# Top-32 attention with an ELU feed-forward block: issuing in the written order in place of the scheduler's, with key and query transposes cut into three parts

## The chip, the cores and the metric

The kernel runs on one core of a Trainium2 chip. Five engines work in parallel, each through its own queue, in order: TensorE (PE, matmuls and transposes; PEld is its weight load), VectorE (DVE), ScalarE (ACT), GpSimd (POOL) and SyncE (SP), which here only issues DMAs. An engine waits where the instruction at the head of its queue waits for a semaphore; nothing behind it can pass. The metric is the device time of the core in microseconds, the median of several executions.

## The reference

```python
def _attn_ref(q, k, v):                      # 8 batches, 8 heads, 576 positions, 64 dims
    scores = scale * np.matmul(q, k.transpose(0, 1, 3, 2))
    kth = np.partition(scores, -32, axis=-1)[..., -32:-31]
    scores = np.where(scores >= kth, scores, -1000000000.0)
    scores = scores - np.max(scores, axis=-1, keepdims=True)
    attn = np.exp(scores)
    attn = attn / (np.sum(attn, axis=-1, keepdims=True) + 1e-09)
    return np.matmul(attn, v)

def _moe_ref(x, w_in, w_out):                # x: 4608 x 512; w_in 512 x 2048, w_out 2048 x 512
    h = x @ w_in
    g = np.where(h > 0.0, h, np.exp(np.minimum(h, 0.0)) - 1.0)
    return g @ w_out
```

In every row of 576 scores only the 32 largest go into the softmax. The two weight matrices arrive as 64-bit floats, which the kernel itself turns into 32-bit ones.

## The kernel before, in words

**Steps.** The attention is cut into 144 steps. A step is one tile of 128 query rows and one pair of heads, so two rows of scores per partition, 128 x 576 each (18 steps per batch: eight for each pair of query tiles, two for the 64 rows left over). What a step needs is spread over several turns of the main loop (L569 to L614). In turn n the code writes down: `scores` of step n+2 (PE matmuls L269, ACT evictions L277); `select` of step n, once for each of its two rows (L281); `mask` of step n-1 (L302); `turn` of step n-2, the transposes of its probabilities (L332); and, where a group of two steps is done, `attend` (L354). `normalise` of step n-1 (L319) stands near the end of the turn. Steps 0 to 7 (`tight`) have a loop of their own, in which a step is masked in its own turn.

**Select** is the work of VectorE: for each of the two rows four MAX8 (L287 and L297, the next eight largest) and three MATCH_REPLACE8 (L291, which strike them out), each reading what the one before it wrote. The two rows have a work tile each (`wk`, two buffers).

**Mask and normalise.** GpSimd negates the 32nd largest value (`neg`, L311) and forms `gap`; ScalarE runs Prelu (L314) and Exp with a running sum (L315); GpSimd adds a small number to the sum (`dene`, L324), VectorE takes the reciprocal (`rec`, L326) and GpSimd multiplies both rows by it (L328).

**Feed-forward.** Rows are gathered into 18 blocks of 128, 256 or 384 rows. A block is 16 `hidden` pieces (L414: matmuls, ScalarE Relu and Exp, and later one VectorE operation, the gate L405) and four `project` pieces per 128 rows. `feed` (L530) is called four times in a step and pops pieces by a planner: each has a cost, each block has a due time, and the work is spread evenly over the steps. `feed` first closes the gates of the pieces popped before, so a gate stands a quarter of a step behind its matmuls. The last block can only start when the last step is attended.

**Decoding of the weights.** 32 pieces of 512 KB are loaded through three `raw` buffers. `hook` (L189), called twice in each select, runs one piece: `convert_first` (three ScalarE operations, L165 to L167, and a GpSimd clamp, L168) and `convert_last` of the piece before it (two VectorE operations, L175 and L178, and a GpSimd sum, L182). Blocks other than the first wait for all 32 pieces.

**Order.** What is written down is not the order in which the engines issue. A scheduler, which runs when the program is built, takes the instructions with their dependences and a model of their costs and sets up each engine's queue. So it can pull an instruction ahead of others that were written before it: in the queue of VectorE it runs the two rows of a select side by side, and it lets a `select` begin ahead of the decoding that was written before it.

Keys and queries are loaded per head pair and turned by `transpose_qk` (L234: ten transposes and three ScalarE copies), 5, 3, 1 and -1 steps ahead of a batch's first step.

Of the kernel before, what the change touches and what calls it, by code (L numbers as in the profile page):

```python
# [10 lines left out]
FP32 = mybir.dt.float32  # L11
# [69 lines left out]
def kernel(  # L81
# [10 lines left out]
    P = nc.NUM_PARTITIONS  # L92
# [7 lines left out]
    NC = dm // P  # L100
    NF = dff // P
    NG = NF // 2
    T = 3 * P
# [14 lines left out]
    xtpool = pool("xt", 2)  # L118
# [5 lines left out]
    late = {}  # L124
# [30 lines left out]
    def convert_first(i):  # L155

        lo, hi, e, m = parts(raw[i])
        ef, mf = e.bitcast(FP32), m.bitcast(FP32)
        nc.scalar.activation(ef, hi.bitcast(FP32), AF.Abs, scale=2.0**-48)  # L165
        nc.scalar.activation(mf, lo, AF.Copy, scale=2.0**-29, bias=2.0**23)
        nc.scalar.activation(m.bitcast(I32), mf, AF.Copy, bias=-(2.0**23))  # L167
        nc.gpsimd.tensor_scalar(  # L168
            ef, ef, (2.0 - 2.0**-3 - 2.0**-23) * 2.0**-32, 2.0**-63, ALU.min, ALU.max
        )  # L170
# [18 lines left out]
    def hook():  # L189

        if not decode:
            return
        decode.pop(0)()
        if not decode:
            raws.close()
            late["g"] = ctx.enter_context(tc.tile_pool(name="g", bufs=2))

    def decode_piece(i):
        if i < 2 * NF:
            if i + 2 < 2 * NF:  # L200
                load_weight(i + 2)
            convert_first(i)
        if i > 0:
            convert_last(i - 1)
            decoded[0] = i

    loaded, kqT, vT = {}, {}, {}

    def load_qk(b, hp):
        for name, src in (("k", k), ("q", q)):  # L210
            t = ldpool.tile([P, J + 1, 2, D], FP32, tag=name + "in", name=name + "in")
            for hh in range(2):
                nc.sync.dma_start(
                    t[:, 0:J, hh, :],
                    src[b, 2 * hp + hh, 0:JP, :].rearrange("(p j) d -> p j d", j=J),
                )
            nc.sync.dma_start(
                t[0:R, J, :, :],
                src[b, 2 * hp : 2 * hp + 2, JP:S, :].rearrange("h p d -> p h d"),
            )  # L220
            loaded[b, hp, name] = t
# [10 lines left out]
        vT[b, hp] = t  # L232

    def transpose_qk(b, hp):  # L234
        d = kvpool.tile([P, 2, S], FP32, tag="kqT", name="kqT")
        kqT[b, hp] = d
        srcs = [loaded.pop((b, hp, name)) for name in ("k", "q")]
        for i, src in enumerate(srcs):
            ps = ps_t.tile([P, JP], FP32, tag="t", name="qkps")
            for c in range(J):  # L240
                nc.tensor.transpose(
                    ps[:, c * P : (c + 1) * P],
                    src[:, c, :, :].rearrange("p h d -> p (h d)"),
                    ident[:],
                )
            nc.scalar.copy(d[:, i, 0:JP], ps[:])
        ps = ps_t.tile([P, JP], FP32, tag="t", name="qkps")
        for i, src in enumerate(srcs):
            nc.tensor.transpose(
                ps[:, i * R : (i + 1) * R],  # L250
                src[0:R, J, :, :].rearrange("p h d -> p (h d)"),
                ident[0:R, 0:R],
            )
        nc.scalar.copy(
            d[:, :, JP:S], ps[:, 0 : 2 * R].rearrange("p (a s) -> p a s", a=2)
        )

    def scores(u):
        q0 = u.t.qt * P
# [42 lines left out]
    def mask(u, i):  # L302

        if u.masked:
            return
        if i == 0:
            u.den = small.tile([P, 2], FP32, tag="den", name="den")
        u.masked = i == 1
        sc, low, top = u.sc[:, i, :], u.last[:, i, 7:8], u.first[:, i, 0:1]
        neg = small.tile([P, 1], FP32, tag="neg", name="neg")  # L310
        nc.gpsimd.tensor_scalar_mul(neg[:], low, -1.0)  # L311
        gap = small.tile([P, 1], FP32, tag="gap", name="gap")
        nc.gpsimd.tensor_tensor(gap[:], low, top, ALU.subtract)
        nc.scalar.activation(sc, sc, AF.Prelu, bias=neg[:], alpha=STEEP)  # L314
        nc.scalar.activation(  # L315
            sc, sc, AF.Exp, bias=gap[:], accum_out=u.den[:, i : i + 1]
        )
# [14 lines left out]
    def turn(u, chunks):  # L332

        if u.turned:
            return
        g = u.group
        if g.et is None:
            g.et = etpool.tile([P, 2 * J + 1, len(g.tiles), P], FP32, tag="et", name="et")
        ps = ps_t.tile([P, JP], FP32, tag="t", name="eps")
        sc = u.sc[:, :, :].rearrange("p i s -> p (i s)")  # L340
        n = chunks.stop - chunks.start
        for c in range(n):
            c0 = (chunks.start + c) * P
            nc.tensor.transpose(ps[:, c * P : (c + 1) * P], sc[:, c0 : c0 + P], ident[:])  # L344
        nc.scalar.copy(  # L345
            g.et[:, chunks, u.at, :],
            ps[:, 0 : n * P].rearrange("p (c q) -> p c q", c=n),
        )
        if chunks.stop == 2 * J + 1:
            u.turned = True  # L350
            if u.at == len(g.tiles) - 1:
                closing.append(g)
# [38 lines left out]

    def finish(blk, parts, at, cols, src):
        if blk.xT is None:
            blk.xT = xtpool.tile([P, NC, T], FP32, tag="xT", name="xT")
        nc.scalar.copy(blk.xT[:, at, cols], src)  # L395
        blk.left -= parts
        if blk.left == 0:
            ffn.extend(ffn_pieces(blk))
# [117 lines left out]
    def at(step, fn, *args):  # L516
        todo.setdefault(step, []).append((fn, args))

    for b in range(1, B):
        f = first[b]  # L520
        for hp, (ahead, ready, late_v) in enumerate(
            ((7, 5, 2), (5, 3, -2), (3, 1, -2), (1, -1, -3))
        ):
            at(f - ahead, load_qk, b, hp)
            at(f - ready, transpose_qk, b, hp)
            at(f - late_v, load_v, b, hp)

    fed = {"at": 0.0, "sum": 0.0, "over": 0.0}
# [1 line left out]
    def feed(n, share):  # L530

        close_gates()
        fed["at"] = max(fed["at"], n)
        ahead = [(w - fed["sum"]) / (x - fed["at"]) for x, w in due if x > fed["at"]]
        if ahead:
            fed["over"] += max(0.0, share * min(ahead))
        fed["at"] += share
        while ffn and decoded[0] >= ffn[0][1] and 0.5 * ffn[0][0] <= fed["over"]:
            cost, _, piece = ffn.pop(0)
            fed["over"] -= cost  # L540
            fed["sum"] += cost
            piece()

    load_qk(0, 0)
    for i in range(2):
        load_weight(i)
    load_qk(0, 1)
    load_v(0, 0)
    transpose_qk(0, 0)
    scores(steps[0])  # L550
    load_qk(0, 2)
    transpose_qk(0, 1)
    scores(steps[1])
    load_qk(0, 3)
    for hp in range(1, NHP):
        load_v(0, hp)
    decode += [lambda i=i: decode_piece(i) for i in range(2 * NF + 1)]
    at(0, transpose_qk, 0, 2)
    at(1, transpose_qk, 0, 3)

    def step(n):
        return steps[n] if 0 <= n < NS else None
# [6 lines left out]
    for n in range(NS + 3):  # L569
        for fn, args in todo.pop(n, []):  # L570
            fn(*args)
        ahead, cur, prev, done = step(n + 2), step(n), step(n - 1), step(n - 2)
        if ahead:
            scores(ahead)
        if n < tight:
            for i in range(2):
                passes = choose(n, i)
                next(passes)
                if i == 0:
                    while closing:  # L580
                        attend(closing.pop(0))
                elif prev:
                    normalise(prev)
                    turn(prev, slice(0, J))
                    turn(prev, slice(J, J + 1))
                    turn(prev, slice(J + 1, 2 * J + 1))
                feed(n, 0.25)
                next(passes)
                mask(cur, i)
                feed(n, 0.25)  # L590
            continue
        if prev:
            mask(prev, 0)
        passes = choose(n, 0)
        next(passes)
        feed(n, 0.25)
        while closing:
            attend(closing.pop(0))
        next(passes)
        feed(n, 0.25)  # L600
        if prev:
            mask(prev, 1)
        if done:
            turn(done, slice(0, J))
            turn(done, slice(J, J + 1))
        passes = choose(n, 1)
        next(passes)
        feed(n, 0.25)
        if done:
            turn(done, slice(J + 1, 2 * J + 1))  # L610
        next(passes)
        if prev:
            normalise(prev)
        feed(n, 0.25)  # L614
# [36 lines left out]
```

## Time and profile before

| | |
|---|---|
| device time, median of 3 | 1848.46 us (1846.58 to 1849.24) |
| span of the profiled execution | 1845.9 us, 25773 instructions |
| VectorE | 1580.3 us busy, 3376 instructions |
| ScalarE | 1125.8 us busy, 2473 instructions |
| GpSimd | 416.6 us busy, 1078 instructions |
| DMA | 56.20 MB, a mean of 30 GB/s |
| MAX8, L287 and L297 | 1152, 837.2 us in sum |
| MATCH_REPLACE8, L291 | 864, 639.0 us in sum |
| gates, L405 | 288, 117.6 us in sum |

Sums of busy time overlap: on VectorE one instruction's record runs on by some 0.08 us after the next has started, so time is best read from start to start. The first MAX8 starts at 16.3 us, that of step 8 at 148.6, of step 48 at 570.6, of step 72 at 849.8 and of step 143 at 1715.6; the last select ends at 1727.1. What follows, 119 us, is feed-forward work alone.

### The profile page before, as it was taken

The numbers are of one execution on the slowest core, as the hardware profiler recorded it, in microseconds if no ns is written. First come the engines' busy times: TensorE is split into PE (matmuls) and PEld (weight loads), VectorE is DVE, ScalarE is ACT, GpSimd is POOL, SyncE is SP. The second block draws the span as 40 slices with busy tenths as digits, with TensorE's granted clock in tenths as the row PEclk, the third lists the DMA queues.
The fourth block names the chain that finished last, engine by engine and source line by source line (L and its number), as shares of the span: only waits on it lengthen the run. The fifth ranks groups of instructions, "written<-read, shape, count | busy, mean of one in ns | idle before, by whom it ended". The sixth has DMA issues, their size and how long they took to land.

```text
span 1845.9 us, 25773 instructions
## 1 busy us (share of the span) xinstructions
PE 1698.4 (92%) x8352; PEld 1025.0 (56%) x8352; DVE 1580.3 (86%) x3376; ACT 1125.8 (61%) x2473; POOL 416.6 (23%) x1078
## 2 busy tenths in 40 slices
PE   5478899999999999999989999999999999899999
PEld 3245656474665655555456565645546465555555
DVE  6889999999999989989889798988989888998400
ACT  5786766676766666667556575657656475665421
POOL 2663222222222221212222221221222212121100
PEclk7579999999999999999999999999999999999999
DMA  5530120001000120001100101001100000000000
GB/s 159 167 126 30 26 56 2 12 20 45 26 7 7 32 58 7 7 24 41 26 12 1 38 23 41 1 12 39 33 19 6 19 20 26 6 7 7 1 18 12
DMA packets 101126, 56.20 MB, mean 30 GB/s; under 512 B 84096, under 2 KB 92288, under 8 KB 100992
## 3 DMA queue, kind: packets, MB, share of 16 engines
q1 hardware_dynamic: 100992, 54.55, 10.6%
q8 instruction: 67, 1.10, 0.2%
q14 instruction: 67, 0.55, 0.1%
HBM read 45.09 MB, written 9.44 MB: 30 GB/s over the span
## 4 chain that ended last, share of the span: by engine, by line
DVE 59%; PE 17%; ACT 12%; issue 3%; POOL 2%; DMA 0%; POOLq 0%; ACTq 0%
DVE wk L291 25%; DVE m L297 22%; DVE m L287 8%; PE hps L425 6%; PE ops L443 6%; ACT sc L314 4%; DVE gT L405 3%; ACT sc L315 3%; ACT sc L277 2%; PE scps L269 2%; PE avps L371 2%; PE eps L344 1%; POOL neg L311 1%; ACT n L434 1%; ACT n L433 1%
## 5 line engine op out<-in xcount | busy, mean ns | idle before, releaser
L297 DVE MAX8 m<-wk 128x8 f32<-128x576 f32 x864 | 628.2, 750 | 4.6
L425 PE MATMUL hps<-xT,w_in 128*128 128x256 f32 (+2 forms) x2304 | 573.5, 395 | 27.8 <-DVE gT L405 26.9
L443 PE MATMUL ops<-w_out,gT 128*128 128x512 f32 x1152 | 535.3, 604 | 1.8 <-DVE gT L405 1.8
L425 PEld LDWEIGHTS hps<-xT,w_in 128*128 128x128 f32 x2304 | 405.5, 196 | 142.4 <-DVE gT L405 45.6
L291 DVE MATCH_REPLACE8 wk<-m,wk 128x576 f32<-128x576 f32 x576 | 426.3, 742 | 0.0
L314 ACT ACTIVATE sc<-sc,neg 128x576 f32<-128x576 f32 x288 | 223.3, 775 | 276.8 <-POOL neg L311 275.6
L443 PEld LDWEIGHTS ops<-w_out,gT 128*128 128x128 f32 x1152 | 208.1, 192 | 208.1 <-issue 199.7
L345 ACT COPY et<-eps 128x512 f32<-128x512 f32 (+1 forms) x432 | 193.5, 476 | 153.5 <-PE eps L344 153.3
L269 PE MATMUL scps<-kqT 64*128 64x64 f32 (+3 forms) x1280 | 244.1, 461 | 25.0 <-ACT sc L277 24.3
L344 PE MATMUL eps<-ident,sc 128*128 128x128 f32 x1296 | 208.0, 284 | 49.3 <-ACT xT L395 16.4
L344 PEld LDWEIGHTS eps<-ident,sc 128*128 128x128 f32 x1296 | 159.6, 144 | 162.3 <-issue 55.2
L311 POOL TENSOR_SCALAR neg<-m 128x1 f32<-128x1 f32 x288 | 62.0, 215 | 831.1 <-DVE m L297 830.0
L328 POOL TENSOR_SCALAR sc<-sc,rec 128x576 f32<-128x576 f32 x288 | 215.7, 759 | 138.9 <-DVE rec L326 130.9
L287 DVE MAX8 m<-sc 128x8 f32<-128x576 f32 x288 | 209.0, 748 | 31.6 <-ACT sc L277 29.6
L315 ACT ACTIVATE sc<-sc,gap 128x576 f32<-128x576 f32 x288 | 223.1, 775 | 16.7 <-ACT sc L314 1.1
L291 DVE MATCH_REPLACE8 wk<-m,sc 128x576 f32<-128x576 f32 x288 | 212.7, 742 | 0.0
L371 PE MATMUL avps<-et,vT 128*64 128x256 f32 (+5 forms) x2000 | 205.5, 337 | 7.0 <-ACT et L345 6.6
L405 DVE SCALAR_TENSOR_TENSOR gT<-n,hps 128x256 f32<-128x256 f32 (+2 forms) x288 | 117.6, 409 | 106.0 <-ACT n L434 104.8
L433 ACT ACTIVATE n<-hps 128x256 f32<-128x256 f32 (+2 forms) x288 | 109.4, 380 | 149.2 <-PE hps L425 146.3
L269 PEld LDWEIGHTS scps<-kqT 64*128 64x128 f32 (+1 forms) x1280 | 114.7, 184 | 143.7 <-issue 109.7
L277 ACT ACTIVATE sc<-scps 128x576 f32<-128x576 f32 x288 | 171.3, 640 | 11.1 <-PE scps L269 11.0
L371 PEld LDWEIGHTS avps<-et,vT 128*64 128x64 f32 (+1 forms) x2000 | 114.0, 140 | 97.4 <-issue 42.2
(34 smaller groups left out, 722.4 us busy)
## 6 DMA issues: line engine op xcount, KB each, us to landing
kin<-in_k_dram SPq DMA_DIRECT2D x64, 128.0 KB, 2.8
qin<-in_q_dram SPq DMA_DIRECT2D x64, 128.0 KB, 2.8
raw<-in_moe_w_in_dram SPq DMA_DIRECT2D x16, 512.0 KB, 4.1
vT<-in_v_dram SPq DMA_DIRECT2D x64, 128.0 KB, 2.3
raw<-in_moe_w_out_dram SPq DMA_DIRECT2D x16, 512.0 KB, 3.2
out_dram<-osb SPq DMA_DIRECT2D x32, 256.0 KB, 2.2
kin<-in_k_dram SPq DMA_DIRECT2D x32, 32.0 KB, 2.5
qin<-in_q_dram SPq DMA_DIRECT2D x32, 32.0 KB, 2.5
```

Source lines behind the costliest of these rows:

```text
L269: nc.tensor.matmul(ps[rows, start[i] : start[i] + keys.stop - keys.start], kq[part, 1, q0 : q0 + u.t.ql], kq[part, 0, keys], start=True, s ...
L277: nc.scalar.activation(u.sc[:, i, :], ps[:, first[i] : first[i] + S], AF.Copy, scale=scale)
L287: nc.vector.max(m, sc)
L291: nc.vector.match_replace(wk[:], m, cur, TAKEN)
L297: nc.vector.max(m, cur)
L314: nc.scalar.activation(sc, sc, AF.Prelu, bias=neg[:], alpha=STEEP)
L315: nc.scalar.activation(sc, sc, AF.Exp, bias=gap[:], accum_out=u.den[:, i : i + 1])
L328: nc.gpsimd.tensor_scalar(u.sc[:, i, :], u.sc[:, i, :], rec[:, i : i + 1], 1.0, ALU.mult, ALU.mult)
L344: nc.tensor.transpose(ps[:, c * P : (c + 1) * P], sc[:, c0 : c0 + P], ident[:])
L371: nc.tensor.matmul(ps[i * D : (i + 1) * D, cols], vt[rows, 2 * J if c == J else i * J + c, :], w, start=(c == 0), stop=(c == J),)
L425: nc.tensor.matmul(ps[:, 0:n_tok], w_in[:, i, f * P : (f + 1) * P], blk.xT[:, i, 0:n_tok], start=(i == 0), stop=(i == NC - 1),)
L443: nc.tensor.matmul(blk.o[:], blk.gT[f // NG][:, f % NG, s * P : (s + 1) * P], w_out[:, f, :], start=(f == 0), stop=(f == NF - 1),)
```

## The change

Four engines (PE, ACT, DVE and POOL) are taken out of the scheduler's hands and issue in the order in which the code is written; SP's queue is still scheduled. The rest of the change fits the written order to that. `transpose_qk` becomes a generator in three parts, of which one is written down at each of three places in a step, one step earlier than before, so that the transposes do not stand in one lump in PE's queue. In `decode_piece` the sum of the piece before is written ahead of the clamp of the next. A block of 128 rows takes its `xT` tile from a pool of its own once decoding is over, so that no copy waits for a block that is written later.

```diff
     def decode_piece(i):
         if i < 2 * NF:
             if i + 2 < 2 * NF:
                 load_weight(i + 2)
-            convert_first(i)
         if i > 0:
             convert_last(i - 1)
             decoded[0] = i
+        if i < 2 * NF:
+            convert_first(i)
...
             nc.scalar.copy(d[:, i, 0:JP], ps[:])
+            yield
...
+    def start_qk(b, hp):
+        turning.append(transpose_qk(b, hp))
+
+    def turn_qk(whole=False):
+        while turning:
+            if next(turning[0], turning) is turning:
+                turning.pop(0)
+            elif not whole:
+                return
...
         if blk.xT is None:
-            blk.xT = xtpool.tile([P, NC, T], FP32, tag="xT", name="xT")
+            if blk.slots == 1 and late:
+                blk.xT = late["x"].tile([P, NC, P], FP32, tag="xT", name="xT")
+            else:
+                blk.xT = xtpool.tile([P, NC, T], FP32, tag="xT", name="xT")
...
-            ((7, 5, 2), (5, 3, -2), (3, 1, -2), (1, -1, -3))
+            ((8, 6, 2), (5, 4, -2), (3, 2, -2), (2, 0, -3))
         ):
             at(f - ahead, load_qk, b, hp)
-            at(f - ready, transpose_qk, b, hp)
+            at(f - ready, start_qk, b, hp)
...
+    E = mybir.EngineType
+    ctx.enter_context(
+        tc.manual_schedule(engines={E.PE, E.Activation, E.DVE, E.Pool})
+    )
...
+        if n < tight:
+            turn_qk(True)
         if ahead:
             scores(ahead)
...
         feed(n, 0.25)
+        turn_qk()
         while closing:
             attend(closing.pop(0))
...
             mask(prev, 1)
+        turn_qk()
...
             turn(done, slice(J + 1, 2 * J + 1))
+        turn_qk()
```

More of the change, by code (lines that the diff above doesn't have):

```diff
@@ L196, in hook @@
             late["g"] = ctx.enter_context(tc.tile_pool(name="g", bufs=2))
+            late["x"] = ctx.enter_context(tc.tile_pool(name="x", bufs=1))
     def decode_piece(i):
@@ L256, in transpose_qk @@
         )
+        yield
+    def start_qk(b, hp):
[6 more added lines that the diff above has]
+                return
+    turning = []
     def scores(u):
@@ L548 @@
     load_v(0, 0)
-    transpose_qk(0, 0)
+    start_qk(0, 0)
+    turn_qk(True)
     scores(steps[0])
     load_qk(0, 2)
-    transpose_qk(0, 1)
+    start_qk(0, 1)
+    turn_qk(True)
     scores(steps[1])
@@ L557 @@
     decode += [lambda i=i: decode_piece(i) for i in range(2 * NF + 1)]
-    at(0, transpose_qk, 0, 2)
-    at(1, transpose_qk, 0, 3)
+    at(0, start_qk, 0, 2)
+    at(1, start_qk, 0, 3)
     def step(n):
@@ L572 @@
         ahead, cur, prev, done = step(n + 2), step(n), step(n - 1), step(n - 2)
+        if n < tight:
+            turn_qk(True)
         if ahead:
```

## The prediction

> **What bounds the kernel now.** I began with the page's first two parts: which engine is full, and when.
>
> ```profile
> PE 1698.4 (92%) x8352; PEld 1025.0 (56%) x8352; DVE 1580.3 (86%) x3376; ACT 1125.8 (61%) x2473; POOL 416.6 (23%) x1078
> ...
> PE   5478899999999999999989999999999999899999
> ...
> DVE  6889999999999989989889798988989888998400
> ```
>
> Both look full, and VectorE stops some 120 us before the end. But a matmul's record is longer than its slot: the group of `hps` 128x256 has a mean of 392 ns, and in the trace one starts 216 ns after the other. Counts by start-to-start times make PE's work about 1520 us (hps 499, ops 494, transposes 176, `avps` 184, `scps` 170). PE has room.
>
> Second, the windows (columns: window, length, then PE, PEld, DVE, ACT, POOL busy, clock, DMA):
>
> ```profile
> 400.00:600.00 200.00, 193.48 (x955) 117.63 (x954) 196.65 (x440) 130.68 (x297) 45.97 (x133) 1.00 0.08 21
> ...
> 1200.00:1400.00 200.00, 190.13 (x854) 104.86 (x853) 174.87 (x364) 118.27 (x248) 40.66 (x117) 0.96 0.09 25
> ...
> 1700.00:1800.00 100.00, 99.35 (x384) 56.21 (x383) 29.04 (x61) 35.13 (x77) 6.30 (x16) 1.00 0.03 9
> ```
>
> Up to step 48 VectorE hardly waits; later it idles one eighth of the time; the end is PE alone. In steps (first MAX8 of each): 10.55 us a step from 8 to 48, 11.63 from 48 to 72, 12.19 from 72 to 143.
>
> Third, VectorE's timeline (start, duration, instruction), because the change touches its order:
>
> ```profile
> 903.97 0.74 DVE L291 MATCH_REPLACE8 wk<-m,wk 128x576 f32<-128x576 f32 x1
> 904.63 0.08 DVE L291 MATCH_VALUE_LOAD wk<-m,wk 128x8 f32 x1
> 904.70 0.74 DVE L291 MATCH_REPLACE8 wk<-m,wk 128x576 f32<-128x576 f32 x1
> 905.36 1.41 DVE L297 MAX8 m<-wk 128x8 f32<-128x576 f32 x2
> 906.80 0.09 DVE L291 MATCH_VALUE_LOAD wk<-m,wk 128x8 f32 x1
> 906.88 0.74 DVE L291 MATCH_REPLACE8 wk<-m,wk 128x576 f32<-128x576 f32 x1
> 907.66 0.76 DVE L297 MAX8 m<-wk 128x8 f32<-128x576 f32 x1
> ```
>
> The scheduler pairs the two rows of a select. Where the neighbours are of different rows, replace to MAX8 takes 0.66 us (904.70 to 905.36); where the second reads what the first wrote, 0.78 (906.88 to 907.66). Medians over the trace, independent and dependent: replace to MAX8 0.659 and 0.776, MAX8 to replace 0.719 and 0.863; MAX8 to anything else 0.669.
>
> The late waits look so (in brackets: idle before, and what ended it):
>
> ```profile
> 1648.01 1.42 DVE L287 MAX8 m<-sc 128x8 f32<-128x576 f32 x2 [0.40 <-ACT sc L277]
> ...
> 1660.76 0.17 DVE L326 RECIPROCAL rec<-dene 128x2 f32<-128x2 f32 x1 [2.49 <-POOL dene L324]
> ```
>
> The chain of waits shows the ring there: last MAX8, `neg`, Prelu, Exp, then the score eviction, queued behind them, then the next MAX8.
>
> Last, the start:
>
> ```profile
> 10.36 0.66 ACT L165 ACTIVATE raw<-raw 128x512 f32<-128x512 f32 x1 [8.36 <-DMA raw<-in_moe_w_in_dram]
> 10.93 1.05 ACT L246 COPY kqT<-qkps 128x512 f32<-128x512 f32 x2
> ...
> 16.31 1.41 DVE L287 MAX8 m<-sc 128x8 f32<-128x576 f32 x2
> ...
> 28.99 1.53 SPq L148 DMA_DIRECT2D raw<-in_moe_w_in_dram  x3
> ...
> 37.85 0.43 DVE L175 TENSOR_SCALAR raw<-raw 128x512 uint32<-128x512 uint32 x1 [1.12 <-POOL raw L168]
> ```
>
> Two pieces are decoded early; the third (37.85) has to wait for its load, issued at 28.99, and meanwhile steps 0 and 1 run.
>
> **The Trainium skill.** "Perfetto Trace Analysis", section "Identifying the Most-Contended Engine", holds matmul busy time for a bad measure of how near PE is to its limit; the 216 against 392 ns agree. "VectorE: DVE Perf Modes", section "The DRAIN you can't avoid", finds that chained VectorE copies cost the same with a semaphore after each as without; for MAX8 and MATCH_REPLACE8 this trace disagrees (0.776 against 0.659), and I take the trace. "SBUF — State Buffer", section "SBUF: two separate sides", says that VectorE and GpSimd can lock each other out of a shared port: L175 took 1.48 us beside a GpSimd sum at 14.19, and 0.43 alone; so I price it at 0.5 to 0.7.
>
> **The change, part by part.**
>
> *VectorE's order.* In the changed build's queue the rows are no longer paired: 864 replace-MAX8 neighbours are all dependent (136 before), and 723 MAX8-replace ones (176 before). Extra: 728 x 0.117 = 85, and 547 x 0.144 = 79. The new queue without any wait: 864 x 0.776 + 723 x 0.863 + 429 x 0.669 (MAX8 before a gate, reciprocal, decoding or the next row) = 670 + 624 + 287; gates 103 (0.195, 0.328, 0.461 by width, plus 0.063 before a replace); reciprocals 16; decoding 32 x 1.3 = 42. Sum 1742. The old queue, priced alike: 1572. After decoding that is 11.8 us a step.
>
> *The ring goes.* Evictions of step n+2 now stand ahead of the masks in ScalarE's queue, two steps before they are read, so the late waits of about 1.3 us a step (12.19 against 10.89 by the same prices) should go. What can still hold VectorE: a gate, if matmul, Relu and Exp aren't done a quarter of a step later. A step with four hidden pieces asks of PE 1.2 for scores, 1.0 for transposes, 0.6 for `attend` and 4 x 1.73: 9.7 us (up to 11 or so with project pieces); of ScalarE 2 x 0.64 evictions, 2 x 1.74 Prelu, Exp and its sum, 1.4 copies of transposes and 4 x 0.8 Relu and Exp: 9.4. Placing a 256-wide step by these durations, the Exp ends some 2.5 us ahead of its gate. The bubble a gate fills between dependent passes is in the prices. I take 20 us for all such waits of steps 8 to 143 (0.15 a step), with 5 and 60 as ends; the trace has no stretch of this order.
>
> *The start.* ScalarE copies keys and queries before it waits for a weight, so step 0 begins near 11.7 (minus 4.6). But in ScalarE's queue three sets of scores stand ahead of the first decoding, and the third waits for its loads: before, its query transposes started at 19.89, its key and query copies ended at 21.3, its matmuls at 22.5; with 1.2 for the eviction 23.7, then L165 0.65 and the clamp 0.6: 25.0. VectorE, done with the first row at about 17.3, waits till then at L175, and all that is queued behind it, the second row and step 1, waits too. Then a ring in each early step: last MAX8 of row 0, 1.2 decoding, 1.3 sum, 0.6 clamp, 0.25 `neg`, 1.75 Prelu and Exp, 0.6 Relu and Exp, 0.65 the next L165, 0.65 clamp, 0.3 `dene`, 0.1: the reciprocal at 7.4, where VectorE is ready at 4.7; the second half of row 1 is queued behind it, and all later work of the step hangs on that. Then 3.2 for this second half, 1.2 decoding, 2.3, 1.2 and 3.2, with gates: 18.7 us a step. Step 8 begins at 25 + 7 x 18.7 + 12 = 168, and some 3 more for gates behind late Exps: about 171 (160 to 180), against 148.6. Sum ahead of clamp is right for the loads (it frees the buffer), and is priced in this ring.
>
> *Transposes in three parts and the earlier loads.* The same instructions: 1.1 us of PE and 1.45 of ScalarE, four times in a batch, hidden behind VectorE's 11.8 us a step, in which both have some 2 us left. Nothing. *xT pool*: no instruction; it keeps a copy from waiting on a later block. Nothing.
>
> *The end.* After the last select PE's queue still holds two `turn`s, one `attend` and about eight project pieces of 3.43 us, in the written order ahead of the last block: some 33 us. The last block from the trace: 2.9 to its first gate, 15 x 1.727, and 30.5 from the last gate's start to the end. Sum 93, against 119 before.
>
> *Sum.* 171 + (1726 - 131 = 1595, step 8 to 143 without waits) + 20 + 11.4 (step 143) + 93 = 1890 of span; the metric was 2.5 above the span: 1893; I say 1890, since some terms are rounded up. Against before: start +22, steps +48, end -26.
>
> **The rivals.** *Faster: the waits were all that mattered.* If the early ring doesn't close and nothing waits, it is 12 + 1736 + 84 (PE never behind) = 1832, with a few us of waits 1840. For it: VectorE idles some 265 us in all now. Against: 170 of that is given back to dependence, and little of the rest is left for a start that waits on loads. 8%. *Even:* early ring half as dear, 0.05 a step: about 1848. 4%. *Much slower: queues in lockstep.* A piece of 3.43 us, or a late normalise ahead of a `turn`, delays PE, Relu and Exp queue behind copies, and every gate waits: 0.7 us a step more makes 1985, 0.4 makes 1945. For it: no queue can now pass its head. Against: PE and ScalarE have 1 to 2 us a step to catch up. 13%. *Main case*, slower by 1 to 4%: 75%.
>
> **The numbers.** Time 1890, the main case. Range 1853 to 1940: the ends of start and waits give 1865 to 1930; it stretches towards both rivals, leaving out 8% of faster and about as much of lockstep. Faster 0.09, same 0.04, slower 0.87.
>
> **What would show it.** Right: VectorE's idle between steps 8 and 143 falls below 30 us while a step takes 11.8 to 12; neighbours at 0.776 and 0.863; the reciprocal of the early steps idle for 2 to 3 us behind `dene`; step 8 near 170; last select to end near 93. Wrong: dependent neighbours nearer 0.66, step 8 before 155, or gates waiting on Exp in every step.

## The result, and the profile after

The changed kernel takes 1967.32 us (median of 4, 1966.95 to 1967.51) against 1848.29 before: a ratio of 1.0645, with a 95% interval of 1.0626 to 1.0663. It is 119 us slower. The forecast had the side right and the size wrong: 1890 was predicted, and 1967 lies above the range's end of 1940.

The page of the changed kernel, first two parts:

```profile
PE 1684.4 (86%) x8352; PEld 1022.5 (52%) x8352; DVE 1690.7 (86%) x3376; ACT 1151.8 (59%) x2473; POOL 404.6 (21%) x1078
...
PE   3436788898889989898898998988899898989999
...
DVE  4878999998899999998899989998989989998800
```

The same instructions; VectorE is busy 110 us longer with them, and still its share is 86%, for the span has grown too. PE's slices are thinner in the middle than before (8 in places where 9 stood).

Two windows of the changed kernel, the same as were shown of before (columns: window, length, then busy time of PE, PEld, DVE, ACT, POOL, clock, DMA):

```profile
400.00:600.00 200.00, 177.18 (x937) 111.99 (x938) 181.20 (x367) 119.83 (x270) 37.39 (x111) 0.97 0.09 24
1200.00:1400.00 200.00, 180.72 (x936) 105.62 (x932) 180.33 (x357) 119.33 (x255) 37.49 (x112) 0.99 0.08 22
```

Between 400 and 600 us VectorE was idle for 3 us and PE for 7 before; now they are idle for 19 and 23. Neither of the two that could be the limit is full any longer. From step 8 to 48 a step takes 12.21 us (before 10.55), from 72 to 143 it takes 12.58 (before 12.19), so most of the loss is where VectorE hardly waited before. PE's granted clock does not explain it: in the second window it was 0.99, before 0.96, and the steps there are longer all the same.

VectorE's timeline of the changed kernel (start, duration, instruction):

```profile
863.85 0.74 DVE L308 MATCH_REPLACE8 wk<-m,wk 128x576 f32<-128x576 f32 x1
864.62 0.76 DVE L314 MAX8 m<-wk 128x8 f32<-128x576 f32 x1
865.42 0.09 DVE L308 MATCH_VALUE_LOAD wk<-m,wk 128x8 f32 x1
865.50 0.74 DVE L308 MATCH_REPLACE8 wk<-m,wk 128x576 f32<-128x576 f32 x1
866.27 0.76 DVE L314 MAX8 m<-wk 128x8 f32<-128x576 f32 x1
```

Each instruction reads what the one before it wrote: 0.77 us from replace to MAX8, 0.88 from MAX8 to replace. Over the whole trace the medians are 0.777 (864 pairs) and 0.874 (0.857 where the MAX8 is a row's first).

PE's waits in the changed kernel between 175 and 1866 us (who waited for whom: us in total, times, longest):

```profile
PE eps L361 <- ACT et L362: 82.3, 63, 4.0
PE eps L361 <- ACT kqT L249: 52.0, 28, 2.5
PE hps L445 <- DVE gT L425: 30.1, 40, 2.2
PE eps L361 <- ACT xT L415: 3.7, 2, 2.3
```

The same view of the kernel before, from 148 to 1727 us:

```profile
PE hps L425 <- DVE gT L405: 21.0, 25, 1.9
PE eps L344 <- ACT xT L395: 16.4, 13, 2.9
PE qkps L249 <- ACT kqT L246: 11.5, 11, 3.9
PE eps L344 <- ACT et L345: 9.6, 14, 1.3
PE qkps L241 <- ACT et L345: 6.2, 6, 1.9
```

The transposes of probabilities (`eps`) now wait 138 us in sum for ScalarE to copy out a PSUM tile; before it was 26 (44 with the waits of the key and query transposes, `qkps`, which use the same tiles; in the changed kernel those are under 2). VectorE's own waits in that stretch:

```profile
DVE gT L425 <- ACT n L454: 57.5, 50, 4.6
DVE rec L343 <- POOL dene L341: 21.5, 14, 3.0
```

From start-to-start times, the account against before is: start +26 (step 8 begins at 175.1, before 148.6); VectorE's waits from step 8 to the last select -39 (84, before 123; the lines above come to 79, because there the overlap of records is left out); VectorE's time without waits there, which is what remains, +152; the end -20 (98.7 from the last select, before 119). That makes up the 119.7 by which the span grew. How the middle 113 part into waits and work is good to some 5 us only.

### The profile page after: what moved, and what is told of

The parts are those of the page before. It is cut to its first block, busy times and chain, and to the rows that moved or that the text cites. A ratio compares the mean times of both kernels' runs of the same rounds, so it can differ in the third digit from the quotient of the medians.

```text
span 1965.6 us, 25639 instructions
## 1 busy us (share of the span) xinstructions
PE 1684.4 (86%) x8352; PEld 1022.5 (52%) x8352; DVE 1690.7 (86%) x3376; ACT 1151.8 (59%) x2473; POOL 404.6 (21%) x1078
## 4 chain that ended last, share of the span: by engine, by line
PE 53%; DVE 26%; ACT 13%; issue 5%; POOL 2%; ACTq 0%; POOLq 0%
PE ops L463 19%; PE hps L445 16%; DVE wk L308 11%; DVE m L314 10%; PE avps L388 7%; PE scps L286 5%; PE eps L361 5%; ACT sc L331 4%; ACT sc L332 3%; DVE m L304 3%; DVE gT L425 2%; ACT et L362 2%; ACT n L454 1%; ACT n L453 1%; ACT sc L294 1%
## 5 line engine op out<-in xcount | busy, mean ns | idle before, releaser
L314 DVE MAX8 m<-wk 128x8 f32<-128x576 f32 x864 | 657.5, 761 | 29.4
L463 PE MATMUL ops<-w_out,gT 128*128 128x512 f32 x1152 | 542.4, 617 | 0.0
L361 PE MATMUL eps<-ident,sc 128*128 128x128 f32 x1296 | 215.8, 291 | 215.4 <-ACT et L362 86.1
L463 PEld LDWEIGHTS ops<-w_out,gT 128*128 128x128 f32 x1152 | 215.9, 197 | 231.6 <-issue 224.8
L341 POOL TENSOR_SCALAR dene<-den 128x2 f32<-128x2 f32 x144 | 32.6, 226 | 959.4 <-ACT sc L332 958.9
L304 DVE MAX8 m<-sc 128x8 f32<-128x576 f32 x288 | 215.3, 748 | 11.7 <-ACT sc L294 11.7
L286 PE MATMUL scps<-kqT 64*128 64x512 f32 (+3 forms) x1280 | 195.9, 454 | 1.0 <-ACT kqT L249 1.0
L388 PE MATMUL avps<-et,vT 128*64 128x256 f32 (+5 forms) x2000 | 194.1, 332 | 0.0
L286 PEld LDWEIGHTS scps<-kqT 64*128 64x128 f32 (+1 forms) x1280 | 102.8, 183 | 130.5 <-issue 126.4
L388 PEld LDWEIGHTS avps<-et,vT 128*64 128x64 f32 (+1 forms) x2000 | 108.8, 137 | 77.2 <-issue 37.1
```

Source lines behind the costliest of these rows:

```text
L286: nc.tensor.matmul(ps[rows, start[i] : start[i] + keys.stop - keys.start], kq[part, 1, q0 : q0 + u.t.ql], kq[part, 0, keys], start=True, s ...
L304: nc.vector.max(m, sc)
L314: nc.vector.max(m, cur)
L388: nc.tensor.matmul(ps[i * D : (i + 1) * D, cols], vt[rows, 2 * J if c == J else i * J + c, :], w, start=(c == 0), stop=(c == J),)
L463: nc.tensor.matmul(blk.o[:], blk.gT[f // NG][:, f % NG, s * P : (s + 1) * P], w_out[:, f, :], start=(f == 0), stop=(f == NF - 1),)
```

## The experiments

**The rest of the change alone.** The scheduler orders all engines again; everything else of the change stays.

```diff
-    E = mybir.EngineType
-    ctx.enter_context(
-        tc.manual_schedule(engines={E.PE, E.Activation, E.DVE, E.Pool})
-    )
```

> The rest of the change (transposes in three parts, loads a step earlier, sum ahead of clamp, own xT pool) with the scheduler still ordering all engines. Theory D (the written order costs through VectorE's order): the rest is worth nothing, 1840 to 1860 us, and replace to MAX8 neighbours stay mixed as before. Rival R (the three parts and the earlier loads load PE's and ScalarE's queues): 1880 us or more.

Measured: 1834.43 us, ratio to before 0.9927 (0.9912 to 0.9943). The rest is not the cost; it is a small gain. So all 119 us, and 14 more, come with the written order. Which of the parts makes the gain was not tried.

**Rows of a select side by side.** The written order stays on four engines, but from step 8 on the two rows alternate.

```diff
+    def select_pair(u):
...
+        for r in range(TOP_K // 8 - 1):
+            for i in range(2):
+                nc.vector.match_replace(wk[i][:], m[i], cur[i], TAKEN)
...
+            for i in range(2):
...
+                nc.vector.max(m[i], cur[i])
...
-        passes = choose(n, 0)
+        passes = select_pair(cur) if cur else iter((None,) * 4)
...
-        passes = choose(n, 1)
```

> The written order kept on four engines, but from step 8 on the two rows of a select are written side by side, so that neighbours on VectorE are of different rows. VectorE needs 9.7 us a step without gates instead of 11.3. Theory D (dependent neighbours are the cost): 1967 falls by 100 to 180 us, to 1790 to 1865; the step after step 8 goes from 12.4 to about 11.2, then set by PE. Rival P (PE and ScalarE in lockstep set the step at about 12 anyway): not below 1930, and VectorE waits at gates and reciprocals for over 200 us.

Measured: 1938.95 us, ratio 1.0495 (1.0478 to 1.0511), 28 us below the changed kernel. The rival holds. VectorE needs some 195 us less from step 8 on, and spends most of it waiting (its waits from 175 to 1800 us):

```profile
DVE rec L370 <- POOL dene L368: 120.0, 50, 5.6
DVE gT L452 <- ACT n L481: 112.7, 81, 5.7
```

So in the changed kernel something other than VectorE sets the step as well.

**The second mask behind the first transposes.** One block moves in the written order of a step, from step 8 on.

```diff
-        if prev:
-            mask(prev, 1)
         turn_qk()
         if done:
             turn(done, slice(0, J))
             turn(done, slice(J, J + 1))
+        if prev:
+            mask(prev, 1)
```

> In steps from 8 on, the second mask of the step before is written behind the first five transposes of probabilities and the second part of the key transposes, so that ScalarE empties their PSUM tiles before it runs that Prelu and Exp. Theory C (the 84 us that VectorE waits after step 8 come from PE standing 138 us behind PSUM copies that are queued behind Prelu and Exp): PE's waits for those copies fall below 70 us, VectorE's waits to about 40, time to 1915 to 1940. Rival L (the waits come from PE's own load in stretches of project pieces): 1955 to 1975, PE's waits fall but the gates wait as before. Also possible: the reciprocal waits more, since its sum ends 0.9 us later.

Measured: 1896.34 us, ratio 1.0260 (1.0244 to 1.0276): 71 us come back, more than the 27 to 52 that I expected. How the wait arises can be read in the changed kernel's timeline (in brackets: idle before, and what ended it):

```profile
885.49 0.60 PE L244 MATMUL qkps<-ident,qin 128*128 128x128 f32 x4
...
885.69 0.59 ACT L472 COPY osb<-ops 128x512 f32<-128x512 f32 x1 [2.50 <-PE ops L463]
...
885.92 0.60 PE L361 MATMUL eps<-ident,sc 128*128 128x128 f32 x4
886.17 0.78 ACT L331 ACTIVATE sc<-sc,neg 128x576 f32<-128x576 f32 x1
887.04 0.77 ACT L332 ACTIVATE sc<-sc,gap 128x576 f32<-128x576 f32 x1
...
887.81 0.56 ACT L249 COPY kqT<-qkps 128x512 f32<-128x512 f32 x1
...
888.28 0.85 ACT L362 COPY et<-eps 128x512 f32<-128x512 f32 x2
...
888.52 0.30 PE L361 MATMUL eps<-ident,sc 128*128 128x128 f32 x1 [2.00 <-ACT kqT L249]
```

The transposes have two PSUM tiles. One is full at 886.1, with queries, the other at 886.5, with probabilities. ScalarE, which has only just been let go by PE's last project piece (its copy `osb`, 885.69), runs Prelu and Exp first because they were written first; the two copies start 1.7 and 1.8 us after their tiles were full, and PE stands still for 2.0 us. The same place with the mask moved:

```profile
873.54 0.60 PE L361 MATMUL eps<-ident,sc 128*128 128x128 f32 x4
873.79 0.59 ACT L249 COPY kqT<-qkps 128x512 f32<-128x512 f32 x1
874.26 0.86 ACT L362 COPY et<-eps 128x512 f32<-128x512 f32 x2
874.52 0.30 PE L361 MATMUL eps<-ident,sc 128*128 128x128 f32 x1 [0.38 <-ACT kqT L249]
...
875.02 0.78 ACT L331 ACTIVATE sc<-sc,neg 128x576 f32<-128x576 f32 x1
```

0.38 us instead of 2.00. From 175 to 1800 us PE's waits for the three kinds of copies fall from 135 to 49 us (those at gates rise from 29 to 66: VectorE is the slower one now), and VectorE's waits nearly vanish:

```profile
DVE gT L425 <- ACT n L454: 15.6, 17, 2.1
DVE rec L343 <- POOL dene L341: 2.6, 5, 1.2
```

What ScalarE has to do ahead of each gate is the same in both orders, only mask and copies have changed places. So what the gates gain comes through PE, which is let go earlier.

**VectorE's order given back to the scheduler.**

```diff
-        tc.manual_schedule(engines={E.PE, E.Activation, E.DVE, E.Pool})
+        tc.manual_schedule(engines={E.PE, E.Activation, E.Pool})
```

> Only VectorE's order goes back to the scheduler; PE, ScalarE and GpSimd issue as written. Theory D: the scheduler pairs rows again and 80 to 150 us come back (1815 to 1890). Rival P: the written order of PE and ScalarE is the cost, so 1930 or more.

Measured: 1931.99 us, ratio 1.0457 (1.0438 to 1.0476). 35 us come back, little more than with the rows side by side, and from other places: step 8 begins at 142.9 instead of 175.1, steps 8 to 143 take 12.19 us instead of 12.45, and the end is longer by 24 us (123 instead of 99). The scheduler pairs the rows only in part: 232 of the neighbours from replace to MAX8 are dependent, where before had 136 and the changed kernel 864. From 175 to 1800 us VectorE waits for evictions (106 us) and gates (49 us). The time is the rival's.

**Both edits together.** Rows side by side and the second mask behind the first transposes.

> Both edits together: the two rows of a select side by side from step 8 on, and the second mask behind the first transposes. Theory S (two limits lie in series: the PSUM copies hold PE and so the step at 12.2; with them loosened, dependent neighbours on VectorE hold it at 11.9): pairing is worth 60 to 100 us now, where it was worth 28 alone; 1800 to 1835 us, steps from 8 to 143 at about 11.2, set by PE's own load. Rival P2 (PE and ScalarE hold the step at about 11.8 for another reason): 1875 or more.

Measured: 1825.54 us, ratio to before 0.9877 (0.9857 to 0.9898). It is 1.2% below the kernel before and, by 9 us, below the rest of the change alone. Pairing was worth 28 us alone and is worth 71 here: the slower of two limits sets the step, and loosening one shows in full only where the other has been loosened too. Steps 8 to 143 take 11.41 us each, in the changed kernel 12.45.

**Transposes of keys and queries in one piece**, at the first of their three places.

```diff
-        turn_qk()
+        turn_qk(True)
         while closing:
             attend(closing.pop(0))
```

> The changed kernel, but the transposes of keys and queries written in one piece, at the first of their three places. Theory C: ScalarE's copies of the PSUM tiles are what PE waits for, 28 times for a key copy in either form, so one piece costs about the same: 1955 to 1985 us. Rival T (the three parts are what makes the written order bearable): 2000 us or more.

Measured: 2013.83 us, ratio 1.0899 (1.0880 to 1.0917). My expectation falls, the rival holds: in the written order the three parts are worth 47 us. Between 175 and 1800 us PE now waits 53 us for key copies at L253, 28 times, as it did for them elsewhere, and 96 for copies of probabilities:

```profile
PE eps L361 <- ACT et L362: 96.2, 74, 3.7
PE qkps L253 <- ACT kqT L249: 53.0, 28, 4.9
```

These two totals grow by 18 us only (79.6 and 52.0 in that stretch of the changed kernel), while VectorE's waits from step 8 on grow by 46 (130 us, 84 in the changed kernel), as much as the time. A lump that hits one quarter of a step, and that quarter's gates, would explain the difference; this was not tested.

**Only the second part of the key transposes ahead of the mask.**

```diff
+        turn_qk()
         if prev:
             mask(prev, 1)
-        turn_qk()
         if done:
```

> The changed kernel, with only the second part of the key and query transposes ahead of the second mask; the transposes of probabilities stay behind it. Theory C: PE's waits for key copies (52 us in 28 places) fall to about 13, those for the copies of probabilities (82 us) stay; the time falls by 15 to 35 us of the 71 that moving both was worth. Rival: the key copies stand in steps with room, so that nothing changes (1962 to 1972).

Measured: 1959.16 us, ratio 1.0597 (1.0576 to 1.0619): 8 us of the 71, less than I expected. PE's waits for key copies fall from 52 to 12.7 us as forecast, but those for copies of probabilities rise from 82 to 96: PE arrives sooner at the next tile, which is still behind the mask. These waits can't be added up as costs.

**The early steps: normalising written half a step sooner** (steps 0 to 7).

```diff
                     while closing:
                         attend(closing.pop(0))
+                    if prev:
+                        normalise(prev)
                 elif prev:
-                    normalise(prev)
```

> The changed kernel, but in steps 0 to 7 the normalising of the step before is written after the first pass of the first row, not of the second. Theory E (in each early step VectorE's reciprocal stands 2.5 us behind a sum that GpSimd forms behind the clamp of a piece): its wait falls to about 1 us, step 8 starts near 164 instead of 175, and the time falls by about 11 us to 1956. Rival (the loads or ScalarE's decoding set the pace of the early steps): step 8 stays at 175, 1967.

Measured: 1976.82 us, ratio 1.0696 (1.0676 to 1.0716), 9 us slower than the changed kernel; step 8 begins at 183.0. Neither expectation holds. Of the changed kernel, the predicted wait is there:

```profile
88.84 0.17 DVE L343 RECIPROCAL rec<-dene 128x2 f32<-128x2 f32 x1 [2.44 <-POOL dene L341]
```

and of this one:

```profile
83.44 0.61 POOL L168 TENSOR_SCALAR raw<-raw 128x512 f32<-128x512 f32 x1 [1.44 <-issue]
84.12 0.23 POOL L341 TENSOR_SCALAR dene<-den 128x2 f32<-128x2 f32 x1
...
84.38 0.17 DVE L343 RECIPROCAL rec<-dene 128x2 f32<-128x2 f32 x1 [3.79 <-POOL dene L341]
```

The sum (`dene`) stands behind a clamp at its new place too, and that clamp waits for ScalarE's L165 (82.64 to 83.30). The wait has moved and grown.

**The clamp ahead of the sum, as it was.**

```diff
             if i + 2 < 2 * NF:
                 load_weight(i + 2)
+        if i < 2 * NF:
+            convert_first(i)
         if i > 0:
             convert_last(i - 1)
             decoded[0] = i
-        if i < 2 * NF:
-            convert_first(i)
```

> The changed kernel with the clamp of a piece ahead of the sum of the piece before, as it was. My ring has clamp and sum on GpSimd one after the other ahead of the negated value either way: step 8 within 6 us of 175, the time within 8 of 1967. Rival (freeing the load buffer earlier was what the edit is for, and the loads would now hold ScalarE): step 8 at 185 or later, 1977 or more.

Measured: 1979.45 us, ratio 1.0714 (1.0698 to 1.0730); step 8 begins at 191.8. In the written order the edit is worth 12 us. These are the numbers of the rival, but not for its reason: up to step 8 ScalarE waits 1.8 us for loads (3.2 in the changed kernel). One cause is in this kernel's timeline:

```profile
66.16 0.61 POOL L168 TENSOR_SCALAR raw<-raw 128x512 f32<-128x512 f32 x1 [2.84 <-issue]
66.73 1.27 POOL L182 TENSOR_TENSOR w_in<-raw 128x512 int32<-128x512 int32 x1
66.80 1.48 DVE L175 TENSOR_SCALAR raw<-raw 128x512 uint32<-128x512 uint32 x1 [0.36 <-POOL raw L168]
```

The sum now follows the clamp at once and runs beside VectorE's L175, which takes 1.48 us; in the changed kernel it takes 0.41 to 0.43, since the sum comes after it. The lock between VectorE and GpSimd that the Trainium skill describes ("SBUF — State Buffer", section "SBUF: two separate sides") agrees: L175 ends at 68.28, just behind the sum (68.00). VectorE's two decoding operations, L175 and L178, take 45.0 us in sum here and 35.3 in the changed kernel, some 10 of the 17 us at step 8 if none of it fell into a wait. In the reciprocal's place the sum stands ahead too, and VectorE waits 2.92 there (2.44). The rest of the 17 us was not taken apart.

**On top of both edits: an early normalising and a later decoding.** Hooks of steps 0 and 1 do nothing, and the normalising of steps 0 to 7 is written sooner, as above.

```diff
+    waiting = [False] * 40 + [True] * 8
...
-        if not decode:
+        if not decode or waiting.pop():
             return
...
+                    if prev:
+                        normalise(prev)
                 elif prev:
-                    normalise(prev)
```

> Pairing, second mask behind the first transposes, the early normalising, and the decoding begun two steps later (hooks of steps 0 and 1 do nothing). Theory: on top of pairing and mask it takes 10 to 25 us from the start, step 8 near 155: 1780 to 1815 us, faster than both kernels. Rival: a later end of decoding holds back feed-forward work, and the end grows by as much as the start shrinks: no difference from the pair of edits.

Measured: 1826.23 us, ratio 0.9886 (0.9868 to 0.9905): no different from both edits alone, as the rival had it. Its reason was not the right one: the end is as long as before the edit (98.0 us). Step 8 begins at 160.0 instead of 176.3, but step 16 at 260.2 against 261.5, since decoding goes on into steps 8 to 10.

**On top of both edits: the normalising a quarter of a step later.**

```diff
         next(passes)
+        if done:
+            normalise(done)
         feed(n, 0.25)
         turn_qk()
...
         next(passes)
-        if prev:
-            normalise(prev)
         feed(n, 0.25)
```

> Pairing and the second mask behind the first transposes, and the normalising of a step written a quarter of a step later, behind the first pass of the next turn. Theory N (with both, VectorE waits 102 us at reciprocals whose sum comes from that second mask, and PE has room): those waits fall below 20 us and the time from 1826 to 1750 to 1790. Rival G (PE's own load and the gates hold the step at 11.4): the wait moves to gates, 1815 or more. In the transposes of the probabilities PE may wait for the later multiplication on GpSimd.

Measured: 1827.18 us, ratio 0.9891 (0.9875 to 0.9908). The rival holds: from step 8 to the last select (176 to 1726 us) VectorE's waits at reciprocals fall from 92 to 34 us, those at gates rise from 35 to 99, and steps 8 to 143 still take 11.4 us. So with both edits it is not VectorE's work alone that sets the step; whether PE's load does was not tested.

## Why the prediction was wrong

By its own sum, term by term: the start, 171 predicted and 175 measured; steps 8 to 143 without waits, 1595 and about 1597 (1680.5 from first MAX8 to first MAX8, less 84 of waits); the waits of these steps, 20 and 84; the last step, 11.4 and 11.3; the end, 93 and 98.7. Of the 76 us by which the span exceeds 1890, 64 are one term.

*Dependent neighbours.* Right to the size: 864 pairs at 0.777 and 723 at 0.86 to 0.87 us. The pairing experiment shows that this is a limit, worth 71 us once the other limit is loosened, and only 28 before.

*The step that failed* is the one on what can still hold VectorE, "Placing a 256-wide step by these durations, the Exp ends some 2.5 us ahead of its gate", and the 20 us of waits that followed from it, where 84 were measured. It placed the engines' work by load, and gave PE and ScalarE 1 to 2 us a step to catch up. It had left out that they also wait for each other through the two PSUM tiles of the transposes: PE can't start the third group until ScalarE has copied the first, and in ScalarE's written order the copy stands behind Prelu and Exp of the second mask, 1.75 us. That took PE 138 us, about 1 us a step and so the lower end of the room it was credited with, and part of the lost time came back as a late matmul, Relu and Exp at a gate. Moving the second mask behind the first transposes took VectorE's waits to about 18 us and the time to 1896: the 20 us and the 1890 of the forecast are what the order gives with most of that wait gone. The mechanism is shown by that run; that a third PSUM tile would do the same is only argued.

*Transposes in three parts, priced at nothing.* Wrong for the same reason. Each part takes one of the two tiles; 28 of them held PE for 52 us, though taking 39 of these away brought only 8. But parts are much better than a lump (47 us), which the prediction hadn't seen either, having counted only busy time.

*The ring goes.* Right for the evictions, which no longer hold VectorE after step 8 (none in its list of waits; before they held it 31 times, 29.6 us in sum). The reciprocal still did, 21.5 us (before 66).

*The start.* Right within 4 us, in part by luck. The first MAX8 was predicted at 11.7 and starts at 11.75. At L175 VectorE waits from about 17.4 to 24.36 (25.0 predicted), and the reciprocal's wait in the early steps is 2.4 us (2.7). But the early steps do not keep one pace: three of the seven after step 1 take 18.2 to 18.3 us, as the ring says with its 18.7, the other four 21.1 to 21.5, and step 1 began 2 us sooner than the sum has it. Both trials of the ring missed their expectation too: the normalising written sooner cost 9 us, and the clamp ahead of the sum, which the ring prices alike, cost 12.

*The rivals.* What came is between the two forms of the lockstep: 0.62 us of waits a step from 8 to 143, where the main case had 0.15, the lighter lockstep 0.55 and the heavier 0.85. Given 13%, it deserved more: "no queue can now pass its head" was the right reason, and nothing in the profile of before could bound it, because there the scheduler had kept those waits at 26 us. The range was also narrower than it seems: the ends of start (180) and waits (60) add up to 1939, not to the 1930 that was written, so the end at 1940 left nothing for a lockstep.

## What to carry to other kernels

Before an order is fixed by hand, list for each PSUM tile who fills it, who empties it, and what is written between the two on the emptying engine: a copy behind two long activations can hold the filling engine for all of their time (2.0 us at the place shown), whatever the loads say. Put short copies that free a shared tile ahead of long work that nobody waits for soon. And where two chains of dependent instructions run on one engine, write them alternately; but look first for a second limit, or the gain (71 us here) shows only in part (28).

## What the runs showed of the hardware that was not expected

A wait total is no price: taking 39 us of PE's waits away at the key copies brought 14 us more at the next copies and 8 us of time, while taking 87 us away at all of them brought 71. Nor does the busy share tell what relief is worth: in the changed kernel PE and VectorE both show 86%, and taking some 195 us of work off VectorE alone brought 28.
